# Long convolution and mixture of experts on one core: inputs, filter spectrum, V and U kept in blocks, U's stores in four pieces

## The chip, the core and the metric

The kernel runs on one core of a Trainium2 chip. Its time is the device time of one execution in microseconds (us). The core has a matrix engine (TensorE, "PE" in the profile, its weight loads "PEld"), a vector engine (VectorE, "DVE"), a scalar engine (ScalarE, "ACT"), a general engine (GpSimd, "POOL") and a sequencer for transfers (SyncE, "SP"). Sixteen DMA engines move data between the chip's memory (DRAM, HBM) and the on-chip SBUF of 128 partitions. PSUM holds the sums of TensorE.

## The reference

A causal long convolution by FFT, and then a layer of eight experts, in which each token goes to the one with the largest gate:

```
B, S, D = 8, 5696, 128                  # 45568 tokens
Xf = rfft(x, 2*S, axis=1);  Hf = rfft(h, 2*S, axis=0)
y  = irfft(Xf * Hf, 2*S)[:, :S]         # (B, S, D)
x  = y.reshape(B*S, D)
e  = argmax(x @ w_gate)                 # E = 8 experts
out[t] = gate[t] * (relu(x[t] @ w1[e]) @ w2[e])     # F = 1024
```

## The kernel before

The sequence index is split in two, s = i + 48 m with 48 values of i (NB) and 119 of m (MB, padded to 120), and so is the transform. The batches are worked in three groups of 2, 3 and 3 (SPLIT). Each group passes three stages, with a scratch tensor in DRAM between two of them:

- **A** (`steps_a`, L267): for each four i and each batch a tile xt of 120 x 512 is loaded (L292), split into two parts by ScalarE and POOL or VectorE (xc, L283 and L284), and transformed over m by TensorE (L305). The result ut, 120 frequencies q on the partitions, is copied from PSUM (L319), and when all batches of the group are in it, it is stored to U (L298, after `late` has held it for two steps). Two of these ut belong to each four i: c = 0 for the real part, c = 1 for the imaginary part.
- **B** (`phase_b`, L443): for each block of four q the tile uq (96 rows: c and i; four q; all columns) is loaded from U (L461) with the matrices mt (L453). TensorE transforms over i (L517), VectorE multiplies with the filter's spectrum hh (L529 to L538), POOL adds (L544), TensorE transforms back (L553) with the matrices mi, and vt is stored to V (L603). In group 0 hh is computed on the way and saved to HS, and mi is made from mt by transposition; groups 1 and 2 load hh from HS (L468) and mi from the input miq (L464).
- **C** (`phase_c`, L679): vq is loaded from V with q on the partitions (L696), the last transform gives y, and each token is gated, ranked and scattered into the sorted tensor SR (L644).

The experts (`pipeline`, L1244) read the sorted rows in tiles of 256 tokens as soon as a part is complete, with weights that `weights` (L228) has split beforehand from moe_w1 and moe_w2 into WD, and scatter the results to out (L1220).

The order is written out by hand: each stage is a generator, and `run` (L1322) interleaves them by given costs while the program is built. The program then holds one fixed row of instructions for each engine, and each engine works its row in order. Stage A of group 0 runs with the filter's own transform (`phase_h`) and `weights`; A of groups 1 and 2 runs as a guest inside C of the group before (`Guest`, L350). All plain transfers are issued by SP in its row; the scatters by POOL. The program has eight counters for SP's transfers (DMAHW0 to DMAHW7), which they take in turn. Buffers that matter here: five xt, four ut (two for each c), four vq or uq.

Of the kernel before, what the change touches and what calls it, by code (L numbers as in the profile page):

```python
# [13 lines left out]
F32 = mybir.dt.float32  # L14
# [9 lines left out]
NB = 48  # L24
MB = 119
QN = 120
MP = 120
HP = 64
# [9 lines left out]
SPLIT = (2, 3, 3)  # L38
C3 = (False, True, True)
SLOTS = (6, 6, 6)  # L40
# [36 lines left out]
def conv_moe(ctx: ExitStack, tc: tile.TileContext, I, out, B, S, D, E, F, split):  # L77
    nc = tc.nc
    P = 128
    K2 = 2 * NB  # L80
# [10 lines left out]
    dram = pool("dram", 1, DRAM)  # L91
# [40 lines left out]
    class Group:  # L132
        def __init__(self, g, b0, nb):
            self.g, self.b0, self.nb = g, b0, nb
            self.cols = nb * D
            self.nch = -(-self.cols // 512)
            self.cb = nb // self.nch
            self.cw = self.cb * D
            assert self.cb * self.nch == nb
            self.ni = SLOTS[g] // nb  # L140
            while NB % self.ni:
                self.ni -= 1
            self.ns = self.ni * nb
            self.scb = 3 if self.ns % 3 == 0 else 2
            self.scw = self.scb * D
            self.qw = max(1, 512 // self.cols)
            self.qb = 4 if self.cols <= 384 else (3 if self.cols <= 512 else 2)
            self.U = dram.tile([QN, K2, self.cols], F32, name=f"U{g}")
            self.V = dram.tile([QN, K2, self.cols], F32, name=f"V{g}")

    groups, parts = [], []
# [13 lines left out]
        groups.append(gr)  # L165
    for pt in parts[:-1]:
        pt.filled = True
    HS = dram.tile([NB, 2, QN, D], F32, name="HS")
    WD = dram.tile([4, E * P, F], F32, name="WD")

    fcs = const.tile([MP, 2, QN], F32, name="c_fcs")
# [56 lines left out]
    def weights():  # L228
        hf = F // 2
        raws, late = {}, []  # L230

        def load(n):
            if n >= 2 * E:
                return
            e, k = divmod(n, 2)
            raws[n] = sb.tile([P, F], F32, tag="wb", name=f"wraw{n}", bufs=4)
            if k == 0:
                nc.sync.dma_start(raws[n], I["moe_w1"][e])
            else:
                nc.sync.dma_start(  # L240
                    raws[n].rearrange("p (c d) -> p c d", d=D),
                    I["moe_w2"][e].rearrange("(c p) d -> p c d", p=P),
                )

        yield 4000
        load(0)
        for n in range(2 * E):
            e, k = divmod(n, 2)
            load(n + 1)
            raw = raws.pop(n)  # L250
            for u in range(2):
                yield 1500
                sp = sb.tile([P, 2, hf], F32R, tag="hs", name=f"wsp{n}_{u}", bufs=4)
                rh = raw[:, u * hf : (u + 1) * hf]
                nc.scalar.copy(sp[:, 0, :], rh)
                rest_of[0].tensor_tensor(out=sp[:, 1, :], in0=rh, in1=sp[:, 0, :].bitcast(F32), op=ALU.subtract)
                yield 1500
                while late:
                    nc.sync.dma_start(*late.pop(0))
                dst = WD[2 * k + u, e * P : (e + 1) * P, :]  # L260
                late.append((dst, sp.bitcast(F32).rearrange("p a f -> p (a f)")))
        yield 1500
        while late:
            nc.sync.dma_start(*late.pop(0))
        state["prepped"] = True

    def steps_a(gr, tag, bufs):  # L267
        g, nb = gr.g, gr.nb
        srcs = [(I["x"][gr.b0 + b], b) for b in range(nb)]
        tw = 4 * D  # L270
        items = []
        for ig in range(NB // 4):
            for src, b in srcs:
                items.append((ig, src, b))
        xts, uts, xss = {}, {}, {}
        split = A3[g]

        def cut(n):
            if not split or n >= len(items):
                return  # L280
            xt = xts.pop(n)
            xs = sb.tile([MP, 2, tw], F32R, tag="us", name=f"xc{g}_{n}", bufs=2)
            nc.scalar.copy(xs[:, 0], xt)  # L283
            getattr(nc, ALO[g]).tensor_tensor(out=xs[:, 1], in0=xt, in1=xs[:, 0].bitcast(F32), op=ALU.subtract)  # L284
            xss[n] = xs

        def load(n):
            if n >= len(items):
                return
            ig, src, b = items[n]  # L290
            xts[n] = sb.tile([MP, tw], F32, tag="xt", name=f"xt{g}_{n}", bufs=5)
            nc.sync.dma_start(xts[n], src[:, ig * tw : (ig + 1) * tw])  # L292

        banks, late, clock = {}, [], [0]

        def flush(everything=False):
            while late and (everything or late[0][0] <= clock[0] - 2):
                nc.sync.dma_start(*late.pop(0)[1:])  # L298

        def transform(m):  # L300
            n, c = divmod(m, 2)
            banks[m] = ps.tile([P, 512], F32, tag="cx", name=f"pa{g}_{n}_{c}", bufs=4)
            ops = [(fcs[:, c], xts[n])] if not split else [(fcr[:, u, c], xss[n][:, v]) for u, v in PASSES]
            for k, (lhs, rhs) in enumerate(ops):
                done = nc.tensor.matmul(banks[m][:QN, :], lhs, rhs, start=(k == 0), stop=(k == len(ops) - 1))  # L305
            if c == 1:
                (xss if split else xts).pop(n)
            return done.ins

        def store(m):  # L310
            n, c = divmod(m, 2)
            clock[0] = m
            ig, src, b = items[n]
            if b == 0:
                uts[c] = sb.tile([QN, 4, gr.cols], F32, tag=tag, name=f"ut{g}_{ig}_{c}", bufs=bufs)
            srcv = banks.pop(m)[:QN, :].rearrange("p (i d) -> p i d", d=D)
            lo = c * NB + ig * 4
            cp = nc.scalar.copy if c == 0 else nc.vector.tensor_copy
            cp(uts[c][:, :, b * D : (b + 1) * D], srcv)  # L319
            if b == nb - 1:  # L320
                late.append((m, gr.U[:, lo : lo + 4, :], uts[c]))

        def fetch():
            for n in range(4):
                load(n)

        def begin(m):
            if m % 2 == 0:
                load(m // 2 + 4)
                cut(m // 2 + 1)  # L330
            return transform(m)

        return fetch, cut, begin, store, flush, 2 * len(items)
# [58 lines left out]
    def phase_h():  # L392
# [3 lines left out]
        for k in range(4):  # L396
            n = NB // 4
            yield 1000
            nc.sync.dma_start(
                ht[:, k * n : (k + 1) * n].rearrange("p i d -> p (i d)"), I["h"][:, k * n * D : (k + 1) * n * D]  # L400
            )
        ucs, banks, hcs = {}, {}, {}

# [39 lines left out]
    def phase_b(gr, guest=None):  # L443
# [4 lines left out]
        def load_m(qb):  # L448
            q = qb * QB
            if q >= QN:  # L450
                return
            mt = sb.tile([K2, QB, P], F32, tag="xt", name=f"mt{g}_{q}", bufs=5)
            nc.sync.dma_start(mt, I["mq"][:, q : q + QB])  # L453
            mats[qb] = mt

        def load(qb):
            q = qb * QB
            if q >= QN:
                return
            uq = sb.tile([K2, QB, gr.cols], F32, tag="ld", name=f"uq{g}_{q}", bufs=LD if g else 3)  # L460
            nc.sync.dma_start(uq, gr.U[q : q + QB].rearrange("q p c -> p q c"))  # L461
            mi = mibufs[qb % 4]
            for k in range(2 if g else 0):
                nc.sync.dma_start(mi[k * HP : k * HP + NB], I["miq"][k * NB : (k + 1) * NB, q : q + QB, :])  # L464
            if g != 0:
                hhs[qb] = hhbufs[qb % 3]
                for k in range(2):
                    nc.sync.dma_start(hhs[qb][k * HP : k * HP + NB, :, :QB], HS[:, :, q : q + QB])  # L468
            tiles[qb] = (uq, mi)

        mats, hhs, hbank = {}, {}, {}
# [16 lines left out]
        def filt(qb, k0):  # L488
            if g != 0 or qb * QB >= QN:
                return  # L490
            mt = mats[qb]
            if k0 == 0:
                hbank[qb] = ps.tile([P, QB, D], F32, tag="mh", name=f"hp{g}_{qb}", bufs=2)
            nc.tensor.matmul(hbank[qb][:, k0, :], mt[:, k0, :], uht[:, qb * QB + k0], start=True, stop=True)

        def filt_save(qb, m):
            if qb not in hbank:
# [6 lines left out]
            nc.scalar.copy(hh[k * HP : (k + 1) * HP, c2], hp[c2 * HP : (c2 + 1) * HP])  # L504
            if m == 3:
                hbank.pop(qb)
                late.append((clock[0], HS[:, :, qb * QB : qb * QB + QB], hh[:NB, :, :QB]))

        def forward(n):
            q, c = items[n]  # L510
# [168 lines left out]
    def phase_c(gr, guest=None, after=None):  # L679
# [12 lines left out]
        def load(n):  # L692
            if n >= nu:
                return
            vq = sb.tile([QN, 2, NI, gr.cols], F32, tag="ld", name=f"vq{g}_{n}", bufs=LD)
            nc.sync.dma_start(vq, gr.V.rearrange("q (c i) x -> q c i x", c=2)[:, :, n * NI : (n + 1) * NI, :])  # L696
            vqs[n] = vq.rearrange("q c i x -> q c (i x)")

        nsub = ns // cb
# [740 lines left out]
```

## Time and profile before

| | |
|---|---|
| median of 3 runs | 2229.18 us (2226.16 to 2232.99) |
| the profiled execution's own time | 2210.35 us |
| its span | 2208.6 us |
| PE busy | 2068.3 us, 94% |
| VectorE, ScalarE, POOL busy | 70%, 50%, 58% |
| DMA | 486.04 MB, mean 220 GB/s |

The span lies a little within the execution's own time. Times in the views count from the span's start. A stretch A:B is a part of the span; "x" with a number counts instructions. A row of waits names the waiting engine and line, what it waited for, the sum, how often, and the longest. In the order of time of SP a number is the time that issuing takes, not the transfer.

### The profile page before, as it was taken

To read this page: it belongs to the slowest core of one execution; us is meant where nothing else is said; L and a number is where in the kernel's file an instruction comes from. 1 tells how busy PE (TensorE), PEld (TensorE's weight loads), DVE (VectorE), ACT (ScalarE), POOL (GpSimd) and SP (SyncE) were. 2 spreads that over 40 slices of the span, in tenths; PEclk is the share of its full clock that TensorE was granted. 3 is DMA by queue.
4 is the path that set the end of the run, shared out by engine and by line. 5 is a ranking of instruction groups with operands and counts; after the bars stand their busy time and mean duration, and the time that the engine had idled before them with its cause. 6 is when DMAs were issued, how large, how long until landed. Compare 5 with 4: busy or idle time off the path is not lost. (4 is left out here: it accounts for less than half of the span.)

```text
span 2208.6 us, 47032 instructions
## 1 busy us (share of the span) xinstructions
PE 2068.3 (94%) x14198; PEld 1749.8 (79%) x14198; DVE 1555.7 (70%) x3731; ACT 1103.8 (50%) x2359; POOL 1287.0 (58%) x1486
## 2 busy tenths in 40 slices
PE   7899899699999999989999999999998999999997
PEld 5688655466667888876777778988888999999997
DVE  4588745599987788769987885777764555555554
ACT  4588644233334666643443445555544444445453
POOL 5366548776654288882665661688873444444442
PEclk9999999799999999999999999999999999999998
DMA  9989999699997798978898977777644543444430
GB/s 289 298 284 317 319 342 319 181 282 274 272 277 223 232 284 241 260 210 214 247 262 222 258 241 207 201 201 200 190 154 144 165 146 116 147 143 146 140 126 27
DMA packets 255353, 486.04 MB, mean 220 GB/s; under 512 B 33285, under 2 KB 155266, under 8 KB 255099
## 3 DMA queue, kind: packets, MB, share of 16 engines
q1 hardware_dynamic: 231163, 435.93, 66.4%
q0 software_dynamic: 23936, 47.09, 6.9%
q8 instruction: 115, 1.88, 0.4%
q14 instruction: 139, 1.14, 0.2%
HBM read 593.26 MB, written 173.52 MB: 347 GB/s over the span
## 5 line engine op out<-in xcount | busy, mean ns | idle before, releaser
L1152 DVE SCALAR_TENSOR_TENSOR hs<-mh,hs 128x512 fp32r<-128x512 f32 x728 | 501.1, 691 | 389.8 <-ACT hs L1150 384.8
L1144 PE MATMUL mh<-xtb,wb 128*128 128x256 f32 x4368 | 689.9, 294 | 40.5 <-DMA wb<-WD 28.1
L1144 PEld LDWEIGHTS mh<-xtb,wb 128*128 128x128 f32 x4368 | 585.3, 190 | 110.1 <-issue 45.9
L1150 ACT ACTIVATE hs<-mh 128x512 fp32r<-128x512 f32 x728 | 435.0, 598 | 473.1 <-PE mh L1144 465.6
L1165 PE MATMUL ma<-hs,wb 128*128 128x256 f32 x4368 | 654.0, 286 | 7.3 <-DMA wb<-WD 7.2
L1165 PEld LDWEIGHTS ma<-hs,wb 128*128 128x128 f32 x4368 | 567.3, 190 | 8.9 <-DMA wb<-WD 8.5
L644 POOL DMA_INDIRECT SR<-rt,pi x384 | 401.6, 1046 | 195.9 <-PE pa L305 50.5
L1220 POOL DMA_INDIRECT out<-xr x252 | 245.8, 975 | 334.4 <-DVE xr L1183 282.1
L544 POOL TENSOR_TENSOR zt<-zt,xs 128x384 f32<-128x384 f32 (+1 forms) x280 | 297.3, 1071 | 116.5 <-DVE xs L536 84.4
L568 ACT COPY vt<-vp 96x384 f32<-96x384 f32 (+1 forms) x300 | 148.9, 496 | 349.4 <-PE vp L553 342.7
L553 PE MATMUL vp<-zt,mi 128*96 128x384 f32 (+1 forms) x720 | 259.4, 456 | 8.3 <-DVE xs L536 5.4
L517 PE MATMUL xp<-uq,mt 96*128 96x384 f32 (+1 forms) x720 | 261.9, 460 | 2.3 <-ACT vt L568 1.7
L529 DVE TENSOR_TENSOR zt<-xp,hh 128x384 f32<-128x384 f32 (+1 forms) x300 | 174.1, 580 | 58.5 <-PE xp L517 54.4
L553 PEld LDWEIGHTS vp<-zt,mi 128*96 128x96 f32 x720 | 113.2, 163 | 102.1 <-issue 53.0
L1220 POOL DMA_INDIRECT out<-xb x112 | 109.0, 973 | 140.9 <-ACT hs L1150 118.6
L536 DVE SCALAR_TENSOR_TENSOR xs<-xp,hh 64x384 f32<-64x384 f32 (+1 forms) x300 | 175.7, 586 | 6.1
L305 PE MATMUL pa<-xc,fcr 120*120 120x512 f32 x576 | 166.0, 419 | 14.5 <-ACT xc L283 6.3
L534 DVE TENSOR_TENSOR xs<-xp,hh 64x384 f32<-64x384 f32 (+1 forms) x300 | 173.2, 577 | 6.0
L638 POOL TENSOR_TENSOR c_fcs<-c_fcs 120x64 f32<-120x64 f32 (+2 forms) x384 | 156.0, 406 | 11.4
L517 PEld LDWEIGHTS xp<-uq,mt 96*128 96x128 f32 x720 | 123.7, 195 | 33.0 <-issue 12.8
L305 PEld LDWEIGHTS pa<-xc,fcr 120*120 120x120 f32 x576 | 98.2, 186 | 50.1 <-DVE rk L852 8.5
L319 DVE COPY ut<-pa 120x512 f32<-120x512 f32 x96 | 65.9, 687 | 91.1 <-PE pa L305 81.7
(128 smaller groups left out, 2299.0 us busy)
## 6 DMA issues: line engine op xcount, KB each, us to landing
wb<-WD SPq DMA_DIRECT2D x728, 512.0 KB
vq<-V SPq DMA_DIRECT2D x64, 720.0 KB
U<-ut SPq DMA_DIRECT2D x48, 720.0 KB
uq<-U SPq DMA_DIRECT2D x60, 576.0 KB
V<-vt SPq DMA_DIRECT2D x60, 576.0 KB
xr<-SR SPq DMA_DIRECT2D x182, 130.0 KB
xt<-x SPq DMA_DIRECT2D x96, 240.0 KB
hh<-HS SPq DMA_DIRECT2D x120, 192.0 KB
```

What stands on the lines that cost most here:

```text
L305: done = nc.tensor.matmul(banks[m][:QN, :], lhs, rhs, start=(k == 0), stop=(k == len(ops) - 1))
L517: nc.tensor.matmul(xj, mt[:, k0 + j, :], uc.rearrange("p (b d) -> p b d", d=D), start=True, stop=True)
L529: nc.vector.tensor_tensor(out=zt, in0=x3, in1=hv[:, 0].broadcast_to([P] + wide), op=ALU.mult)
L536: nc.vector.scalar_tensor_tensor(out=xs[to], in0=x3[at], scalar=-1.0, in1=him, op0=ALU.mult, op1=ALU.mult)
L544: eng.tensor_tensor(out=zt, in0=zt, in1=xs, op=ALU.add)
L553: nc.tensor.matmul(vp[:K2, j * cw : (j + 1) * cw].rearrange("p (b d) -> p b d", d=D), mi[:, k0 + j, :], zt.rearrange("p b (j d) -> p b j d ...
L644: s = nc.gpsimd.indirect_dma_start(out=SR[:, :], out_offset=IndirectOffsetOnAxis(ap=pi[:, b : b + 1], axis=0), in_=rt[:, b, :], in_offset= ...
L1144: nc.tensor.matmul(hp[:, u, :], wb[:, a, f, :], xt[:, b, :], start=(n == 0), stop=(n == 2))
L1150: done = nc.scalar.activation(hs[:, 0], hp, AF.Relu)
L1152: nc.vector.scalar_tensor_tensor(out=hs[:, 1], in0=hp, scalar=0.0, in1=hs[:, 0].bitcast(F32), op0=ALU.max, op1=ALU.subtract)
L1165: nc.tensor.matmul(accs[t], wb[:, a, f, :], hs[:, b, u, :], start=(k == 0 and u == 0 and n == 0), stop=(k == NPAIR - 1 and u == 1 and n == 2),
L1220: sc = nc.gpsimd.indirect_dma_start(out=out[:, :], out_offset=IndirectOffsetOnAxis(ap=xr[:, s, D + 1 : D + 2].bitcast(I32), axis=0), in_=x ...
```

## The change

Every tensor in DRAM that a stage reads is laid out in the order of the reads, so that what one transfer reads is one block, or one run per partition. For the inputs x, h, mq, miq and moe_w2 the host does it. HS and U become blocks of four q. In groups 1 and 2 the rows of V are put in another order by the columns of miq, so that a vq tile reads one run of each partition; group 0 reads V as before. U's block has the four q next to each other, while ut has q on the partitions: the columns of fcs are permuted so that partitions 0 to 29 hold the first of each four frequencies, 30 to 59 the second, and so on, and ut is stored in four transfers of 30 partitions.

```diff
-            self.U = dram.tile([QN, K2, self.cols], F32, name=f"U{g}")
+            self.U = dram.tile([QN // 4, K2, 4, self.cols], F32, name=f"U{g}")
-    HS = dram.tile([NB, 2, QN, D], F32, name="HS")
+    HS = dram.tile([QN // 4, NB, 2, 4, D], F32, name="HS")
...
-                    I["moe_w2"][e].rearrange("(c p) d -> p c d", p=P),
+                    I["moe_w2"][e].rearrange("p (c d) -> p c d", d=D),
...
-            nc.sync.dma_start(xts[n], src[:, ig * tw : (ig + 1) * tw])
+            nc.sync.dma_start(xts[n], src[ig])
...
-                late.append((m, gr.U[:, lo : lo + 4, :], uts[c]))
+                n = QN // 4
+                for k in range(4):
+                    late.append((m, gr.U[:, lo : lo + 4, k], uts[c][k * n : (k + 1) * n]))
...
-            nc.sync.dma_start(mt, I["mq"][:, q : q + QB])
+            nc.sync.dma_start(mt, I["mq"][qb])
-            nc.sync.dma_start(uq, gr.U[q : q + QB].rearrange("q p c -> p q c"))
+            nc.sync.dma_start(uq, gr.U[qb])
-                nc.sync.dma_start(mi[k * HP : k * HP + NB], I["miq"][k * NB : (k + 1) * NB, q : q + QB, :])
+                nc.sync.dma_start(mi[k * HP : k * HP + NB], I["miq"][qb, k])
-                    nc.sync.dma_start(hhs[qb][k * HP : k * HP + NB, :, :QB], HS[:, :, q : q + QB])
+                    nc.sync.dma_start(hhs[qb][k * HP : k * HP + NB], HS[qb])
...
-            nc.sync.dma_start(vq, gr.V.rearrange("q (c i) x -> q c i x", c=2)[:, :, n * NI : (n + 1) * NI, :])
+            if g:
+                nc.sync.dma_start(vq.rearrange("q c i x -> q (c i) x"), gr.V[:, 2 * n * NI : 2 * (n + 1) * NI, :])
+            else:
+                nc.sync.dma_start(vq, gr.V.rearrange("q (c i) x -> q c i x", c=2)[:, :, n * NI : (n + 1) * NI, :])
...
+    fcs = fcs[:, :, q.reshape(QN // 4, 4).T.ravel()]
...
-        "x": xp.reshape(B, MP, NB * D),
+        "x": xp.reshape(B, MP, NB // 4, 4 * D).transpose(2, 0, 1, 3),
-        "moe_w2": moe_w2,
+        "moe_w2": moe_w2.reshape(E, F // 128, 128, D).transpose(0, 2, 1, 3).reshape(E, 128, -1),
-        "mq": mqf.transpose(1, 0, 2),
+        "mq": mqf.reshape(QN // 4, 4, 2 * NB, 128).transpose(0, 2, 1, 3),
```

The row of SP in stage A of group 0, before, with the counter or engine that each transfer waits for; xt_8 to xt_11 are tiles of x, ut_1_0 and ut_1_1 the two results of the second four i:

```order
L292 DMA xt_8_210<-x 120x512 [waits DMAHW1_49,Pool_49]
L292 DMA xt_9_226<-x 120x512 [waits DMAHW2_49,Pool_49]
L298 DMA U_70<-ut_1_0_185 120x1024 [waits DMAHW3_49,Activation_49]
L298 DMA U_70<-ut_1_1_198 120x1024 [waits DMAHW4_49,DVE_49]
L292 DMA xt_10_247<-x 120x512 [waits DMAHW5_49,Pool_49]
L292 DMA xt_11_277<-x 120x512 [waits DMAHW6_49,Pool_49]
```

The same place of SP's row in the changed kernel:

```order
L292 DMA xt_8_216<-x 120x512 [waits DMAHW7_49,Pool_49]
L292 DMA xt_9_232<-x 120x512 [waits DMAHW0_49,Pool_49]
L298 DMA U_70<-ut_1_0_185 30x4x256 [waits DMAHW1_49,Activation_49]
L298 DMA U_70<-ut_1_0_185 30x4x256 [waits DMAHW2_49]
L298 DMA U_70<-ut_1_0_185 30x4x256 [waits DMAHW3_49]
L298 DMA U_70<-ut_1_0_185 30x4x256 [waits DMAHW4_49]
L298 DMA U_70<-ut_1_1_201 30x4x256 [waits DMAHW5_49,DVE_49]
L298 DMA U_70<-ut_1_1_201 30x4x256 [waits DMAHW6_49]
L298 DMA U_70<-ut_1_1_201 30x4x256 [waits DMAHW7_49]
L298 DMA U_70<-ut_1_1_201 30x4x256 [waits DMAHW0_49]
L292 DMA xt_10_259<-x 120x512 [waits DMAHW1_49,Pool_49]
L292 DMA xt_11_289<-x 120x512 [waits DMAHW2_49,Pool_49]
```

Two transfers have become eight; a counter comes round after eight transfers, so the one before it must have landed; the places around them are the same.

SP in C of group 0 with A of group 1 (ut of 120 x 1536, vq a tile of V), before:

```order
L298 DMA U_72<-ut_4_0_3004 120x1536
L298 DMA U_72<-ut_4_1_3006 120x1536
L292 DMA xt_21_3308<-x 120x512
L696 DMA vq_9_3340<-V_71 120x2x768
L292 DMA xt_22_3357<-x 120x512
```

The same place in the changed kernel:

```order
L298 DMA U_72<-ut_4_0_3094 30x4x384 x4
L298 DMA U_72<-ut_4_1_3096 30x4x384 x4
L292 DMA xt_21_3410<-x 120x512
L701 DMA vq_9_3442<-V_71 120x2x768
L292 DMA xt_22_3459<-x 120x512
```

Here too two stores have become eight, between the same loads.

## Rows read from the trace of the kernel before

**Rows 1.** Stretches: busy us (instructions) PE, PEld, DVE, ACT, POOL; PEclk, DMA share, GB/s
```profile
0.00:88.00 88.00, 70.52 (x321) 51.67 (x321) 41.47 (x60) 48.23 (x94) 49.10 (x51) 0.94 0.91 298
98.00:262.00 164.00, 155.42 (x854) 130.26 (x855) 130.08 (x188) 127.34 (x232) 95.82 (x76) 0.95 0.95 302
262.00:395.00 133.00, 114.98 (x598) 69.00 (x596) 69.76 (x307) 64.38 (x160) 83.03 (x120) 0.96 0.94 317
434.00:690.00 256.00, 246.99 (x1207) 167.06 (x1207) 242.68 (x466) 90.20 (x200) 163.71 (x177) 0.99 0.99 270
700.00:945.00 245.00, 235.55 (x1749) 203.63 (x1749) 190.16 (x628) 157.07 (x360) 167.69 (x219) 0.99 0.86 250
990.00:1320.00 330.00, 318.38 (x1814) 241.61 (x1813) 293.89 (x555) 130.67 (x270) 177.96 (x185) 0.99 0.87 242
1740.00:2140.00 400.00, 400.00 (x3430) 400.00 (x3430) 226.02 (x397) 199.26 (x395) 191.91 (x198) 1.00 0.42 139
```

**Rows 2.** What SP waited for, 0 to 88: us, times, longest
```profile
SPq L292 <- POOL xc L284: 18.9, 9, 4.7
SPq L298 <- ACT ut L319: 5.2, 2, 3.2
SPq L298 <- DVE ut L319: 4.7, 3, 2.4
```

**Rows 3.** Order of time on SP, 59 to 70: start, us taken, transfer
```profile
59.28 0.79 SPq L298 DMA_DIRECT2D U<-ut  x2
60.17 3.13 SPq L292 DMA_DIRECT2D xt<-x  x2
...
64.12 2.45 SPq L298 DMA_DIRECT2D U<-ut  x2
66.67 2.97 SPq L292 DMA_DIRECT2D xt<-x  x2
69.73 0.83 SPq L298 DMA_DIRECT2D U<-ut  x2
```

**Rows 4.** Single lines: SP's issues, ns min/median/max, first and last start
```profile
L298 SPq DMA_DIRECT2D U<-ut x72: 316/360/2807, 14.5 to 954.1; - x72
...
L292 SPq DMA_DIRECT2D xt<-x x96: 324/426/5950, 1.3 to 918.9; - x96
...
L603 SPq DMA_DIRECT2D V<-vt x90: 312/537/1270, 124.9 to 1331.9; - x90
...
L468 SPq DMA_DIRECT2D hh<-HS x120: 543/547/807, 435.5 to 1295.3; - x120
...
L696 SPq DMA_DIRECT2D vq<-V x64: 843/933/2846, 268.2 to 1580.2; - x64
```

**Rows 5.** The page, DMA issues: transfer, count, KB each
```profile
U<-ut SPq DMA_DIRECT2D x48, 720.0 KB
...
hh<-HS SPq DMA_DIRECT2D x120, 192.0 KB
...
U<-ut SPq DMA_DIRECT2D x24, 480.0 KB
```

**Rows 6.** DMA queue, 741.6 to 744, U stores: packets, MB, share
```profile
q1 hardware_dynamic: 161, 0.87, 94.4%
```

**Rows 7.** DMA queue, 475.8 to 476.4, expert weights
```profile
q1 hardware_dynamic: 73, 0.26, 105.3%
```

**Rows 8.** DMA queue, 474 to 474.6, uq and V
```profile
q1 hardware_dynamic: 153, 0.24, 105.7%
```

**Rows 9.** DMA queue, 193.6 to 194.4, uq and V of group 0
```profile
q1 hardware_dynamic: 240, 0.25, 97.7%
```

**Rows 10.** DMA queue, 198.8 to 199.6, w2
```profile
q1 hardware_dynamic: 421, 0.24, 101.5%
```

**Rows 11.** DMA queue, 711.6 to 713.6, V loads
```profile
q1 hardware_dynamic: 160, 0.45, 97.4%
```

**Rows 12.** DMA queue, 471 to 473, hh loads mostly
```profile
q1 hardware_dynamic: 278, 0.43, 96.8%
```

More of the change, by code (lines that the diff above doesn't have):

```diff
@@ L268, in steps_a @@
         g, nb = gr.g, gr.nb
-        srcs = [(I["x"][gr.b0 + b], b) for b in range(nb)]
+        srcs = [(I["x"][:, gr.b0 + b], b) for b in range(nb)]
         tw = 4 * D
@@ L399, in phase_h @@
             nc.sync.dma_start(
-                ht[:, k * n : (k + 1) * n].rearrange("p i d -> p (i d)"), I["h"][:, k * n * D : (k + 1) * n * D]
+                ht[:, k * n : (k + 1) * n].rearrange("p i d -> p (i d)"), I["h"][k]
             )
@@ L493, in filt @@
                 hbank[qb] = ps.tile([P, QB, D], F32, tag="mh", name=f"hp{g}_{qb}", bufs=2)
-            nc.tensor.matmul(hbank[qb][:, k0, :], mt[:, k0, :], uht[:, qb * QB + k0], start=True, stop=True)
+            nc.tensor.matmul(hbank[qb][:, k0, :], mt[:, k0, :], uht[:, k0 * (QN // QB) + qb], start=True, stop=True)
         def filt_save(qb, m):
@@ L506, in filt_save @@
                 hbank.pop(qb)
-                late.append((clock[0], HS[:, :, qb * QB : qb * QB + QB], hh[:NB, :, :QB]))
+                late.append((clock[0], HS[qb], hh[:NB]))
         def forward(n):
@@ L1393 @@
     mqf = mq.astype(f32)
+    miq = np.stack([mqf[:, :, :NB], mqf[:, :, HP : HP + NB]], 2)
+    ni = SLOTS[1] // SPLIT[1]
+    miq = miq.reshape(QN, 2, NB // ni, ni, 2, NB).transpose(0, 2, 1, 3, 4, 5).reshape(QN // 4, 4, 2 * NB, 2, NB)
     total = (B * S - E) // T + E
@@ L1422 @@
     ins = {
-        "x": xp.reshape(B, MP, NB * D),
-        "h": hp.reshape(MP, NB * D),
+        "x": xp.reshape(B, MP, NB // 4, 4 * D).transpose(2, 0, 1, 3),
+        "h": hp.reshape(MP, 4, NB // 4 * D).transpose(1, 0, 2),
         "moe_w1": moe_w1,
-        "moe_w2": moe_w2,
+        "moe_w2": moe_w2.reshape(E, F // 128, 128, D).transpose(0, 2, 1, 3).reshape(E, 128, -1),
         "fcs": fcs.astype(f32),
-        "mq": mqf.transpose(1, 0, 2),
-        "miq": np.concatenate([mqf[:, :, :NB], mqf[:, :, HP : HP + NB]], 2).transpose(2, 0, 1),
+        "mq": mqf.reshape(QN // 4, 4, 2 * NB, 128).transpose(0, 2, 1, 3),
+        "miq": miq.transpose(0, 3, 4, 1, 2),
         "small": small,
```

## Prediction

> **What bounds the kernel now.** I read the table of stretches first, then what SP waited for, its order of time in the first stage, and last the pace of single kinds of transfers.
>
> In stretches [rows 1]: TensorE (PE) is busy 400.00 of 400 us from 1740 to 2140, when only the experts run. No transfer can shorten that. Before it come stage A of group 0 (0 to 88 us), B of group 0 (98 to 262), C of group 0 with A of group 1 as its guest (262 to 395), B of group 1 (434 to 690), C of group 1 with A of group 2 (700 to 945), B of group 2 (990 to 1320) and C of group 2. The change acts in these. In the two stretches in which U is written first, the DMA engines are busy 0.91 and 0.94, while PE is idle 17.5 of 88 us and 18.0 of 133. In B of group 0 PE is busy 155.4 of 164, in B of group 1 VectorE 242.7 of 256, in B of group 2 PE 318.4 of 330, in C of group 1 PE 235.6 of 245. So where U is read a compute engine is already at 95 to 96%, and where U is written the transfers set the pace.
>
> SP issues every transfer of this kernel but the scatters, in one fixed order. In the first stage it waits mostly for compute: 18.9 us for POOL to free an xt buffer, some 10 us for ut to be filled [rows 2]. In its order of time a turn of two x tiles and two U stores takes about 5.6 us there (59.28 to 64.12 to 69.73), and the xt loads hold SP some 1.5 us each (3.13 and 2.97 us for two) [rows 3], against 0.43 for such an issue in the middle [rows 4]. SP is held when the engines are behind: the sign of a stage at the transfers' limit.
>
> **The change part by part.** On PE, VectorE, ScalarE and POOL nothing moves: their instructions stand in the same order, and their durations don't depend on which row is which frequency. On SP a U store becomes four, nothing else changes place.
>
> *Issue.* There are 24 U stores in each group (24 of 480 KB, 48 of 720 KB [rows 5]), so 72 more issues per group. No row shows a store of 30 partitions. The nearest below is a U store as it is, 0.316 us at least and 0.360 in the middle; the nearest above are the V store, which also writes four runs per partition, 0.537, and the hh load, 0.547 [rows 4]. I take 0.54, since the V store has the same form. That is 96 x 0.54 - 24 x 0.36 = 43 us more of SP's time in each of the three stretches; at 0.32 it would be 22. Back come 0.933 - 0.43 = 0.5 us for each of the 48 V loads of groups 1 and 2 (24 us), and about 0.1 us for each of 120 hh loads and 30 HS stores (15 us), all off the path in stretches where SP has time.
>
> *Engine time.* A transfer's pace is its MB over the length of the window over the share. U stores of 6144 B runs go at 0.87 / 2.4 / 0.944 = 384 GB/s [rows 6], 4096 B at 0.26 / 0.6 / 1.053 = 411 [rows 7], 1536 B at 0.24 / 0.6 / 1.057 = 378 [rows 8], 1024 B at 0.25 / 0.8 / 0.977 = 320 [rows 9], 512 B at 0.24 / 0.8 / 1.015 = 296 [rows 10]. The share of rows 6 is just over 15/16: a transfer of 120 partitions sits on 15 engines, and a piece of 30 may too; so I scale by 15/16 or 16/15 where the kinds differ.
> - U written: group 0 moves 24 x 480 KB = 11.8 MB, now in 1024 B runs: 39.3 us instead of 30.6, 8.7 more. Groups 1 and 2 move 17.7 MB each, in 1536 B runs: 50.0 instead of 46.1, 3.9 more each.
> - U read is the mirror image: group 0 has 11.8 MB in 4096 B runs, 8.2 us less; groups 1 and 2 have 17.7 MB each in 6144 B runs at 410 GB/s, 3.6 less each.
> - w2: 8 x 512 KB in 4096 B runs instead of 512 B: 4 us less, half in A and half in B of group 0.
> - V loads go at 0.45 / 2 / 0.974 = 231 GB/s in 3072 B runs [rows 11], slower than any store, so it is not the run length that holds them back. I take no gain; at the pace of rows 6 the 24 loads of a group, 17.7 MB, would take 46 us instead of 77, the other end, and in C of group 1 PE could use at most its 9.4 idle us of that.
> - The blocks of x, h, mq and miq keep their run lengths. hh and HS go from 2048 to 4096 B, at most a fifth of small amounts. I cost both at nothing; B's compute hides it.
>
> Over the whole kernel the engines' time is a wash (8.7 + 7.8 - 8.2 - 7.2 - 4 = 3 us less). What counts is the place: more where transfers bind, less where compute does.
>
> The Trainium skill ("DMA: Bandwidth & Descriptors", Rules for kernel authors) speaks against this change: small transfers are to be coalesced into one, and splitting one by partition halves brings nothing, since the parts run on the same engines. Here B of group 1, with its 192 KB hh loads [rows 5], still keeps the engines at 0.99 [rows 1], so the trace agrees only in part. By the page's fit of 2 us for each transfer and eight in flight, 216 more would cost, as an estimate, 54 us; the sum goes by the rows above.
>
> *Stage by stage.* A of group 0: SP has to issue 96 pieces (51.8 us) and 41 others at 0.43 (17.6), 69 of 88 us, and waits 29 us for compute as now [rows 2]; with the waits kept in full it ends at 69 + 29 = 98, 10 us late, and with 0.1 us behind each of 137 issues, as between the lines of rows 3, 24 us late. If they are hidden by SP being late itself, nothing is lost there. The engines' 8.7 - 2 = 6.7 us more would just fill their idle tenth (0.91 to 0.99). A turn needs 8 x 0.54 + 2 x 0.43 + 0.43 = 5.6 us of SP, all of the turn of rows 3. Behind the late pieces stand the next xt loads, for which ScalarE's and POOL's cuts wait, then PE. I take 8 us, from 0 to 24. C of group 0: the engines, at 0.94, get 3.9 us more, and pieces that each wait for the transfer eight before them let less be queued while SP waits. I take 5, from 2 to 15. C of group 1: 43 us more of SP in 245, the engines at 0.86; weight loads may stand 4.3 us behind a pair of stores. I take 2, from -9 to 8. B of group 0: 10 us less for the engines (8.2 + 2), but PE is idle only 8.6 us; I take 2 off, at most 8. B of groups 1 and 2: one off each, at most 13 and 12, the idle time of VectorE and of PE there.
>
> Sum: 8 + 5 + 2 - 2 - 2 = 11 us more. The profiled execution took 2210.35 us around a span of 2208.6, so 2221; it lies 19 us under the median of the three runs, 2229.18. On the median: 2240 us.
>
> **The rivals.**
> 1. *The relief in B wins, the kernel is faster.* If the idle time in the three B stages is mostly waiting for transfers, and SP absorbs the pieces (0.32 us each), B gives back 6 + 8 + 6 of its 8.6, 13.3 and 11.6 idle us, A and C lose 8: 12 us less, 2217. For it: the engines are at 0.95 and 0.99 in the first two. Against it: the waits of SP show compute late, not transfers. It decides once B gives back more than the 8 us.
> 2. *Nothing to see.* The pieces are issued within SP's waits, the swap of run lengths cancels: 2229, give or take 5. For it: the sum of engine time is unchanged, and SP's waits are long.
> 3. *Narrow pieces are slow.* The loads of hh, into 48 partitions, go at 0.43 / 2 / 0.968 = 222 GB/s in 2048 B runs [rows 12]. If stores of 30 partitions do too, U takes 53 us instead of 31 in A and 80 instead of 46 in C: some 22 + 30 more (the idle 0.06 of C takes a few us of 34), with C of group 1 hiding its 34 in its idle seventh: 2281. Against it: rows 12 are writes into SBUF and a U store reads it; for it: nothing in the trace isolates a narrow store.
>
> **How the numbers follow.** My forecast 0.42, rival 1 0.20, rival 2 0.22, rival 3 0.16. A change under 0.3% (7 us) cannot be told from none here: faster is below 2222, slower above 2236. Faster 0.2, same 0.22, slower 0.58. The likeliest one's own range is 2232 to 2260. The ends of the stages add up to -40 and +47, but they hardly fall together; the range takes in the first rival and reaches towards the third, which leaves one in ten on each side: 2213 to 2272.
>
> **What would show it.** In the changed profile the U pieces should take SP about 0.54 us each; SP should wait less for POOL's xc in the first 90 us; the first uq load should come up to 10 us later than now; C of group 0 should end some 5 us later still; the B stages should last the same to 2 us with the DMA share down a few hundredths; and PE should run the experts in the end as it does now. If the stretch from the first uq load of group 0 to its last V store is over 5 us shorter, rival 1 holds. If A's engines show far more time per byte of U, rival 3. If A is no longer than before, my main term is wrong.

## The result and the profile after

| | before | after |
|---|---|---|
| median, same chip | 2230.45 us (2226.16 to 2232.99, 6 runs) | 2244.40 us (2240.66 to 2247.58, 6 runs) |
| the profiled execution | 2210.35 us | 2240.93 us |
| its span | 2208.6 us | 2239.1 us |

The changed kernel is slower: the recorded ratio is 1.0075, 95% interval [1.0057, 1.0093]; the medians, 14 us apart, give 1.0063. Here and below the two can differ by about 0.1%. 2240 us was forecast. The two profiled executions lie 30 us apart, twice as far as the medians. Before's median was 2230 us in these runs, and 2228, 2210 and 2231 us on the three chips of the experiments. The profiled execution of before, 2210 us, lies outside the range of its six runs and at the median of the second of those chips, so the rows of before above may come from another chip than those of after. Stage times are therefore compared further below between two kernels profiled on one chip.

The stretches of after, as in [rows 1] (busy us of PE, PEld, DVE, ACT, POOL; clock, DMA share, GB/s):

```profile
0.00:88.00 88.00, 69.46 (x304) 50.57 (x304) 39.31 (x57) 44.66 (x87) 47.71 (x49) 0.92 0.92 280
262.00:395.00 133.00, 103.75 (x514) 62.44 (x513) 65.45 (x263) 59.89 (x147) 75.90 (x108) 0.94 0.97 301
1800.00:2140.00 340.00, 340.00 (x2879) 335.87 (x2877) 189.57 (x332) 164.35 (x332) 160.96 (x167) 1.00 0.42 140
```

The first two are the stretches in which U is written first. The DMA engines are as busy as before or busier (0.92, 0.97) and move less (280 instead of 298 GB/s, 301 instead of 317). The last shows TensorE without a gap when only the experts run, as before, but from 1800 us on; from 1740 to 1800 it was busy 56.8 of 60.

What SP waited for, 0 to 88, as in [rows 2]:

```profile
SPq L292 <- POOL xc L284: 7.9, 4, 4.6
SPq L298 <- DMA xt<-x: 4.1, 6, 1.4
...
SPq L298 <- DMA ht<-h: 2.6, 1, 2.6
...
SPq L298 <- ACT ut L319: 1.4, 3, 0.7
```

The wait for POOL fell from 18.9 to 7.9 us and that for ScalarE's ut from 5.2 to 1.4. New is that the U stores (L298) wait for earlier transfers, of x, h and the weights. These are not data that they need: by the rows of order above it is the counter, whose last transfer has to land first.

The order of time on SP at the place of [rows 3] (start, us taken):

```profile
61.81 4.69 SPq L298 DMA_DIRECT2D U<-ut  x8
66.60 0.83 SPq L292 DMA_DIRECT2D xt<-x  x2
...
67.96 5.63 SPq L298 DMA_DIRECT2D U<-ut  x8
73.69 0.86 SPq L292 DMA_DIRECT2D xt<-x  x2
74.65 4.69 SPq L298 DMA_DIRECT2D U<-ut  x8
```

Before, the xt loads held SP (3.13 and 2.97 us for two) and two U stores went by in 0.8 to 2.5. Now the eight pieces take 4.69 and 5.63 us, and two xt loads 0.83: the time has moved from waiting for compute to the stores. From one pair of stores to the next it took 4.8 and 5.6 us [rows 3]; now it takes 6.2 and 6.7 (61.81 to 67.96, 67.96 to 74.65).

SP's issues by line, as in [rows 4] (ns min/median/max), each from its own line's view:

```profile
L298 SPq DMA_DIRECT2D U<-ut x288: 311/422/1891, 14.4 to 976.6; - x144
...
L699 SPq DMA_DIRECT2D vq<-V x48: 18/409/1467, 723.3 to 1603.4; - x48
...
L470 SPq DMA_DIRECT2D hh<-HS x120: 253/362/1239, 454.8 to 1317.9; - x120
```

A piece takes 0.42 us in the middle; I had taken 0.54. The V loads of groups 1 and 2 went from 0.93 to 0.41, as forecast, and hh from 0.55 to 0.36, nearly twice the gain that was forecast.

The queue of after in 0.8 us (66.0 to 66.8) in which only pieces of group 0 move, and in 1 us (945 to 946) with pieces of group 2 (packets, MB, share):

```profile
q1 hardware_dynamic: 314, 0.28, 102.4%
```

```profile
q1 hardware_dynamic: 257, 0.35, 95.2%
```

That is 0.28 / 0.8 / 1.024 = 342 GB/s in runs of 1024 B and 0.35 / 1 / 0.952 = 368 in runs of 1536 B, beside 320 and 378 for other transfers in runs of that length [rows 9, 8] and 384 for a whole store in runs of 6144 B [rows 6]. Stores of thirty partitions, several of them in flight, are not slow.

### The profile page after: what moved, and what is told of

Read it like the earlier page. It is cut to its first block, busy times and chain, and to the rows that moved or that the text cites. A ratio compares the mean times of both kernels' runs of the same rounds, so it can differ in the third digit from the quotient of the medians.

```text
span 2239.1 us, 47291 instructions
## 1 busy us (share of the span) xinstructions
PE 2080.9 (93%) x14198; PEld 1753.4 (78%) x14198; DVE 1556.1 (69%) x3731; ACT 1101.4 (49%) x2359; POOL 1285.8 (57%) x1486
## 5 line engine op out<-in xcount | busy, mean ns | idle before, releaser
L1225 POOL DMA_INDIRECT out<-xb x112 | 109.2, 975 | 169.7 <-ACT ot L1180 108.6
```

What stands on the lines that cost most here:

```text
L1225: sc = nc.gpsimd.indirect_dma_start(out=out[:, :], out_offset=IndirectOffsetOnAxis(ap=xr[:, s, D + 1 : D + 2].bitcast(I32), axis=0), in_=x ...
```

## The experiments

My theory: U's stores cost because there are four times as many transfers. It has two forms. In theory 1 the time that SP needs to issue them decides, in theory 2 the eight counters that all transfers share. The rivals: the short runs of U's new layout, and the other blocks.

**U as before, the rest changed.**

```diff
-            self.U = dram.tile([QN // 4, K2, 4, self.cols], F32, name=f"U{g}")
+            self.U = dram.tile([QN, K2, self.cols], F32, name=f"U{g}")
...
-                n = QN // 4
-                for k in range(4):
-                    late.append((m, gr.U[:, lo : lo + 4, k], uts[c][k * n : (k + 1) * n]))
+                late.append((m, gr.U[:, lo : lo + 4, :], uts[c]))
...
-            nc.sync.dma_start(uq, gr.U[qb])
+            nc.sync.dma_start(uq, gr.U[q : q + QB].rearrange("q p c -> p q c"))
...
-            nc.tensor.matmul(hbank[qb][:, k0, :], mt[:, k0, :], uht[:, k0 * (QN // QB) + qb], start=True, stop=True)
+            nc.tensor.matmul(hbank[qb][:, k0, :], mt[:, k0, :], uht[:, qb * QB + k0], start=True, stop=True)
...
-    fcs = fcs[:, :, q.reshape(QN // 4, 4).T.ravel()]
```

> The changed kernel with U alone as before (one store per ut, old layout). Theory (the four pieces cost SP's issues and the counters, the rest of the change does nothing): 2226 to 2233 us, ratio to the kernel before 0.997 to 1.001. Rival (the other blocks are slow too, or shift the stages): ratio 1.004 or more. Rival (the other blocks help and U hides it): ratio under 0.996.

Measured: 2225.02 us (12 runs), 0.998 [0.9961, 0.9999] of before. The loss is U's alone; the other blocks together are worth nothing or a little gain.

**U's change alone** (the same lines of the diff, put into the kernel before).

> The kernel before with the change of U alone. Theory: as slow as the changed kernel or a little slower, ratio 1.005 to 1.010, since only U matters. Rival (the other blocks cause the loss): ratio within 0.002 of 1.

Measured: 2237.73 us (8 runs), 1.0051 [1.0033, 1.0068].

**Four transfers, old layout.** Runs of 6144 and 4096 B as before, U and uq as before.

```diff
-                late.append((m, gr.U[:, lo : lo + 4, :], uts[c]))
+                n = QN // 4
+                for k in range(4):
+                    late.append((m, gr.U[k * n : (k + 1) * n, lo : lo + 4, :], uts[c][k * n : (k + 1) * n]))
```

> The kernel before, U's layout and run lengths unchanged, but each U store in four transfers of 30 partitions. Theory (number of issues): most of the loss, ratio 1.004 to 1.009, the stretch up to the first uq load of group 1 some 10 to 20 us longer. Rival (the short runs cost the engines' time, not the issues): ratio within 0.002 of 1.

Measured: 2241.25 us (6 runs), 1.0057 [1.0036, 1.0078], as much as U's whole change. The first uq load of group 1 comes at 453.5 us, beside 436.6 and 442.2 in the fourth and the first experiment, whose stores are whole.

**One transfer, short runs.** A row of U is padded by 64 floats, so that a store writes four runs per partition.

```diff
-            self.U = dram.tile([QN, K2, self.cols], F32, name=f"U{g}")
+            self.U = dram.tile([QN, K2, self.cols + 64], F32, name=f"U{g}")
...
-                late.append((m, gr.U[:, lo : lo + 4, :], uts[c]))
+                late.append((m, gr.U[:, lo : lo + 4, : gr.cols], uts[c]))
...
-            nc.sync.dma_start(uq, gr.U[q : q + QB].rearrange("q p c -> p q c"))
+            nc.sync.dma_start(uq, gr.U[q : q + QB, :, : gr.cols].rearrange("q p c -> p q c"))
```

> The kernel before with U's rows padded by 256 B, so that each U store is still one transfer but writes four runs of 1024 or 1536 B per partition; the loads keep their run lengths. Theory (number of issues): ratio 1.000 to 1.003 (the engines' 8.7 and 3.9 us hardly seen). Rival (run length): ratio 1.005 or more.

Measured: 2227.71 us (12 runs), 1.0003 [0.9987, 1.0019]. These four ran on one chip (before 2227.69 us) and settle the first question: the number of transfers costs, and the length of their runs does not, or by no more than 0.2%.

**SP's time without counters.** Two loads of a register from SBUF (of a 0 in the tile zero) on SP behind each U store of the kernel before.

```diff
...
+                for _ in range(2):
+                    nc.sync.value_load(zero[0:1, 0:1], min_val=0, max_val=1)
```

> The kernel before; behind each of the 72 U stores SP loads a register twice (some 1.3 us of SP's time, about what three further issues take), with no transfer and no counter. Theory 1 (what the pieces cost is SP's issue time): ratio 1.004 to 1.007, as with four pieces. Theory 2 (what they cost is that a counter comes round after eight small transfers, so SP waits for a landing): ratio under 1.002.

Measured: 2239.18 us (6 runs) against 2210.34, on another chip: 1.0129 [1.0096, 1.0162]. The dose was larger than meant (ns min/median/max of what a load consists of):

```profile
L303 SPq TENSOR_LOAD <-zero x144: 271/742/2446, 15.0 to 987.2; - x144
L303 SPq FUSED_REGOPS  x144: 147/147/192, 15.7 to 988.7; - x144
```

Two loads are 1.8 us a store, where the pieces add 4 x 0.42 - 0.36 = 1.3. So it shows that SP's time costs, and not that it costs as much as the pieces. Its 1.29% cannot be set beside the 0.5 to 0.6% above either: the kernel before is 17 us faster on this chip than on the other, four pieces in all groups were not run here, and in time 2239 us is what the kernels with four pieces took there (2238 and 2241).

**Counters with little time.** Three transfers behind each U store whose condition is never true: they move nothing, but each takes its counter (never[0] is a register that holds 0, SK a scratch tensor).

```diff
...
+                for _ in range(3):
+                    nc.sync.dma_start(SK[skips[0]], ident[0:1, :], cond=never[0], cond_hint=False)
...
```

> The kernel before; behind each of the 72 U stores SP has three transfers that are skipped by a register (0.1 us each, nothing is moved), each of which takes the next of the eight counters. Theory 1 (issue time): 0.4 us a store, a third of the pieces' cost at most, ratio under 1.002. Theory 2 (counters): ratio 1.003 to 1.006, and SP's U lines in C of group 0 take some 4 us or more a store as the pieces do.

Measured: 2241.60 us (6 runs), same chip, 1.0143 [1.0112, 1.0174]. SP's order of time in the first stage:

```profile
64.88 0.75 SPq L308 DMA_DIRECT2D SK<-ident  x3
65.72 0.33 SPq L304 DMA_DIRECT2D U<-ut  x1
66.33 3.80 SPq L308 DMA_DIRECT2D SK<-ident  x3
```

Three of them go by in 0.75 us where nothing holds them; at the next place the same three hold SP 3.80 us, and the profile counts 91 us of waits at this line in the whole program. So waiting for counters costs, too. It is more than either theory expected, but it is not the counters alone: the three take 0.75 us of SP even where they are free.

**Two pieces of 60 partitions**, and **four in group 0 alone** (the split of the third experiment with 2 for 4, and under `if g == 0`).

> The kernel before with each U store in two transfers of 60 partitions, run lengths as before. Theory 1 (issue time, one third of the further issues): ratio about 1.002. Theory 2 (counters: eight transfers still hold more than half of the bytes): ratio 1.000 to 1.002. A cost of any splitting as such would give 1.005 again.

> The kernel before with the U stores of group 0 alone in four transfers, those of groups 1 and 2 whole. By the forecast's sizes A of group 0 carries over half of the loss: ratio 1.003 to 1.005. Rival (the loss is in C of group 0 and of group 1, where the transfers between are long): ratio 1.000 to 1.002.

Measured on that chip: 2212.36 us (12 runs), 1.001 [0.999, 1.003], and 2216.72 (12 runs), 1.0024 [1.0004, 1.0044]. One more transfer per store cannot be told from none. That does not show that the cost is out of proportion to the count: a third of 0.57% is 0.19%, inside the interval, so neither theory is ruled out. With four pieces in group 0 alone the kernel loses about 5 us (1 to 10), between the two expectations. The first transform of B comes at 115.9 us here, beside 109.2 with two pieces.

**One register load, and the changed kernel beside the one with U as before.** One load instead of two; and on the same chip, a third one (before 2230.57 us, 29 runs), the changed kernel and the first experiment again.

> Kernel before, with one register load of 0.9 us (742 + 147 + 18 ns in the run with two) on SP behind each of the 72 U stores, which takes no counter. The three additional pieces of a store take 1.2 to 1.4 us of SP when nothing holds them, so this is about two thirds of their time on SP. Theory 1 (the time that SP spends decides): 0.3 to 0.7% slower, 1.003 to 1.007, half of the 1.3% of two loads or a little more than half of the pieces' 0.6 to 0.75%. Theory 2 (the counters decide, and the two loads cost only because they held SP longer than the pieces do): within 0.15% of before, under 1.0015.

> The changed kernel again, so that it, the kernel with U as before and the kernel before stand on one chip. Both theories: 0.5 to 0.9% over before, and 0.6 to 1.0% over the kernel with U alone as before. If this chip is one on which before takes about 2210 us, the first U load of group 0 should come 4 to 8 us later than in before, and C of group 0 should show the part that the slower chip hid: up to 3 us.

> The changed kernel with U's layout and stores as before, once more, beside the changed kernel on the same chip. If the other blocks are worth what the first run showed, 0.996 to 1.000 of before; if that was chance, the interval lies around 1.000. The gain that my engine-time rows give for w2 is 4 us at most (0.998).

Measured, 12 runs each: one load 2239.75 us, 1.0033 [1.0015, 1.0052]; the changed kernel 2240.08, 1.0044 [1.0028, 1.006]; with U as before 2224.73, 0.9973 [0.9954, 0.9991]. The changed kernel is 0.69% over the one with U as before, as expected, and a little less over the kernel before than the 0.5% expected. The load was a little longer here:

```profile
L303 SPq TENSOR_LOAD <-zero x72: 437/935/1818, 15.5 to 976.3; - x72
L303 SPq FUSED_REGOPS  x72: 111/152/192, 16.1 to 977.2; - x72
```

So 1.1 us of SP's time per store, without any counter, cost 0.33% on the chip on which the pieces, at 1.3 us, cost 0.69%. In proportion to their time the pieces would cost 0.4% by that (an estimate), a little over half. SP's time costs by itself; that it accounts for the whole is not shown. The lower end of the interval, 0.15%, is as much as was expected at most if the counters decide. And the load does not act where the pieces do: the first uq load came at 99.0 us, as with U as before (99.1), with the pieces at 102.8, and some 8 us of the loss of the profiled execution lie in B of group 1 (278.9 us beside 271.0), where no U store and so no register load stands. Why, is open. The expected gain of the other blocks was seen twice, and the version with U as before beats both kernels: by 0.27% [0.09, 0.46] the kernel before, by 15 us of the medians the changed one. Which of the other blocks gives the gain was not tried.

## Why the prediction came out, step by step

The stages of two kernels from one chip: the changed kernel, cut at its last transform in A of group 0, the first of B, the last of B, the first of C, and the first uq or vq load of each later stage:

```profile
0.00:90.80 90.80, 71.86 (x318) 51.63 (x318) 39.96 (x59) 46.65 (x92) 48.64 (x50) 0.94 0.91 278
90.80:115.80 25.00, 15.54 (x91) 13.49 (x89) 9.90 (x16) 11.56 (x23) 3.01 (x3) 0.75 0.93 288
115.80:266.10 150.30, 146.38 (x829) 122.27 (x828) 128.57 (x185) 122.96 (x225) 95.87 (x76) 0.98 0.94 305
...
283.50:453.80 170.30, 133.09 (x674) 80.08 (x674) 78.25 (x390) 67.11 (x173) 107.67 (x161) 0.89 0.85 262
453.80:723.10 269.30, 260.79 (x1308) 179.06 (x1308) 253.31 (x485) 97.77 (x216) 170.87 (x184) 1.00 0.96 271
723.10:998.00 274.90, 259.99 (x1915) 223.63 (x1915) 206.07 (x704) 167.82 (x389) 191.55 (x259) 0.98 0.82 235
```

The same stages with U as before, all else changed (so the two differ in U alone, and w2 and the other blocks are in both):

```profile
0.00:88.20 88.20, 71.64 (x317) 52.17 (x318) 40.99 (x59) 47.37 (x93) 48.74 (x50) 0.94 0.90 295
88.20:109.60 21.40, 15.13 (x90) 13.34 (x89) 9.38 (x16) 10.91 (x22) 2.99 (x3) 0.86 0.96 296
109.60:259.80 150.20, 146.26 (x829) 122.15 (x828) 128.61 (x185) 122.88 (x225) 95.84 (x76) 0.99 0.96 308
...
277.30:436.60 159.30, 127.40 (x674) 77.18 (x674) 79.24 (x390) 67.14 (x173) 107.53 (x161) 0.93 0.83 277
436.60:707.50 270.90, 261.76 (x1315) 179.64 (x1315) 253.89 (x486) 98.29 (x217) 170.77 (x184) 1.00 0.97 270
707.50:979.50 272.00, 258.45 (x1907) 223.43 (x1906) 205.29 (x703) 167.50 (x387) 193.67 (x259) 0.98 0.81 237
```

The second number of a row is the length. The changed kernel is 2.6 us longer in A of group 0, 3.6 in the passage to B, 0.1 in B, 0.1 shorter in the row left out (17.4 against 17.5), 11.0 longer in C of group 0, 1.6 shorter in B of group 1 and 2.9 longer in C of group 1; behind that the two differ by less than 1 us until the end of their spans (2239.1 and 2219.8). These are single executions; the medians differ by 15.4. How far other traces bear them out is said with each stage.

- **A of group 0: 8 forecast, 6.2 measured, and only part of it where I put it.** The uq load was 3.7 us late (102.8 against 99.1), by the mechanism that I gave: pieces at SP, next loads late. The turn of 5.6 us that I set the pieces against was the longer of the two in [rows 3]; the other took 4.8. What I had not priced is the passage. SP of the changed kernel, and then of the one with U as before:

```profile
87.28 9.52 SPq L298 DMA_DIRECT2D U<-ut  x16
...
102.22 0.41 SPq L455 DMA_DIRECT2D mt<-mq  x1
102.82 0.58 SPq L463 DMA_DIRECT2D uq<-U  x1
```

```profile
87.03 2.66 SPq L298 DMA_DIRECT2D U<-ut  x2
...
97.59 0.42 SPq L453 DMA_DIRECT2D mt<-mq  x1
99.14 0.34 SPq L461 DMA_DIRECT2D uq<-U  x1
```

  At 87 us the one has sixteen pieces left, 9.52 us, the other two stores, 2.66. The mt loads behind them come 4.6 us late, and TensorE waits for them, 7.9 us instead of 5.1:

```profile
PE hp L496 <- DMA mt<-mq: 7.9, 1, 7.9
```

```profile
PE hp L494 <- DMA mt<-mq: 5.1, 3, 4.5
```

  This stage is the best shown: the first transform of B comes at 115.1 to 117.0 us in all five traces with four pieces in group 0, and at 108.5 to 109.6 in all five with one store or two, on every chip.
- **Issue of a piece: 0.54 taken, 0.42 measured.** The V store was the wrong neighbour for a store of four runs; a U store as it is (0.36) was nearer. By that 43 us more of SP per group are 96 x 0.42 - 24 x 0.36 = 32. Where the DMA engines are behind, the counters add to it: in C of group 0 eight pieces took 9.47 us.
- **C of group 0: 5 forecast, 11 measured in this pair, some 7 over all traces; this is the term that I sized too small.** From the first transform of C to the start of the uq load it took 164.3 to 170.0 us in the four traces with four pieces in every group (mean 167.7), and 159.0 to 164.0 in the three with whole stores on the chips where before takes about 2230 us (mean 160.7); the two ranges almost touch. I took 3.9 us of engine time for U's shorter runs, and a little for the counters. From the packets of the queue in that stage (their times added up, over 16 engines), U's own engine time is 48.0 us instead of 46.3, so 1.7; but the V loads (3072 B, the same in both) took 40.4 instead of 32.0 us, and x 20.6 instead of 19.1. The middle V packet took 160 ns instead of 121. SP, changed kernel first:

```profile
328.14 0.85 SPq L701 DMA_DIRECT2D vq<-V  x1
329.10 1.03 SPq L292 DMA_DIRECT2D xt<-x  x2
330.22 0.85 SPq L701 DMA_DIRECT2D vq<-V  x1
...
332.32 9.47 SPq L298 DMA_DIRECT2D U<-ut  x8
```

```profile
326.57 4.42 SPq L292 DMA_DIRECT2D xt<-x  x2
331.16 1.03 SPq L298 DMA_DIRECT2D U<-ut  x2
332.29 2.05 SPq L699 DMA_DIRECT2D vq<-V  x1
334.44 5.80 SPq L292 DMA_DIRECT2D xt<-x  x2
```

  With whole stores two transfers of 720 KB are handed over in a microsecond and run beside the loads; with pieces SP stands at the eight of them for 9.47 us, in part until earlier transfers have landed, and the loads behind them come in a bunch. After, V loads with little beside them (384.6 to 386.6 us):

```profile
q1 hardware_dynamic: 140, 0.40, 96.8%
```

  0.40 / 2 / 0.968 = 207 GB/s: with little beside them they are as slow as [rows 11] had it (231) or slower, while their mean over the stage with whole stores among them was 325. That the loads lose because they meet each other and no longer stores is my reading of these rows; the runs show that they lose with pieces (40.7 us in U's change alone, 36.8 with the old layout) and not with short runs (32.5, against 34.1 before). They also show that pieces are not needed for it: with whole stores they took 44.8 us where skipped transfers held SP, and 36.1 with one register load. So holding SP is enough to slow the loads, whatever the form of the stores beside them. What SP waited for in C of group 0 (280 to 454 us, changed kernel; 277 to 437, U as before):

```profile
SPq L298 <- DMA vq<-V: 14.0, 7, 3.2
...
SPq L292 <- DVE xc L284: 9.8, 5, 4.4
```

```profile
SPq L292 <- DVE xc L284: 29.8, 8, 7.1
```

  The stores now wait 14.0 us for the V loads whose counters they take, and the 20 us less that SP waits for xc show it late itself. The copies into ut pay for it: who waited for the stores in the whole program, changed kernel and U as before (us, times):

```profile
ACT ut L319: 28.3, 9
DVE ut L319: 28.0, 10
```

```profile
ACT ut L319: 13.1, 4
...
DVE ut L319: 4.6, 2
```

  Of the 11.0 us, 5.3 are idle time of TensorE (37.2 against 31.9), and 5.7 are busy time for the same 674 matmuls, at a mean granted clock of 0.89 instead of 0.93: of its two levels, 1.2 and 2.4 GHz, TensorE was granted the lower one for longer in the stage with more gaps.
- **C of group 1: 2 forecast, 2.9 measured.** The DMA engines had room there (0.82). Other traces show nothing clear: from the first vq load of group 1 to the first uq load of group 2 it took 270.0 to 275.2 us with pieces and 272.0 to 274.8 with whole stores.
- **B: 2, 1 and 1 us off forecast for groups 0, 1 and 2; 0.1 more, 1.6 less and 0.4 more measured** (2 us of engine time for w2 that I counted in group 0 are in both kernels). As said, PE and VectorE bound it. The contiguous uq brought no relief to be seen: the DMA share in B of group 1 is 0.96 instead of 0.97. Rival 1, the relief in B, is gone with that.
- **w2 and the other blocks: 4 us less of engine time forecast.** Measured for all of them together: 2.7 and 5.8 us less of the medians on two chips. Rival 2, nothing to see, would be near the truth for this half of the change.
- **Rival 3, narrow pieces slow: wrong** by the 342 and 368 GB/s above; it had 222.

So the sum of 11 came from the right mechanism: late loads behind the pieces in A and C of group 0. C of group 0 was too small, the issue time and A a little too large, the relief in B did not come, and the other blocks' gain was a little too small. That the total lies within 3 us of the 14 on the medians is in part luck, since these errors offset each other. The rule of the Trainium skill that I weighed ("DMA: Bandwidth & Descriptors", Rules for kernel authors: do not split by partition) pointed the right way. Its fit of 2 us a transfer (section "Anatomy of one DMA — SWDGE (gpsimd) path") is measured on transfers that GpSimd issues, and these are issued by SP; the estimate of 54 us from it was three and a half to five times the 10 to 15 us that U's pieces cost.

What stays open: how the pieces' cost divides between SP's time and the counters. The two traces from one chip tell how SP's own time divides. 96 pieces at 0.42 us are 40 us of issuing in each group, 24 whole stores at 0.34 are 8. The waits of these lines for earlier transfers add up to 10.8 us instead of 3.7 in A of group 0 and to 22.4 instead of 1.9 in C. So of what SP spends more on the pieces, issuing is 32 us in each group and waiting 7 in A and 20 in C of group 0; how much of either ends up in the kernel's time is not shown. Register loads and skipped transfers each cost by themselves (1.29 and 1.43%), but on a chip on which the pieces were not run in all groups.

## What to carry over

Where one queue issues everything in a fixed order, as here, splitting a store was paid at the next loads in that row, and at the passage between stages, not at the store: count the issues between the last store and the first load of the next stage. Two pieces cost nothing that could be measured here (0.1%, from -0.1 to 0.3) and four did; whether the cost sets in at some point or grows with the count is not shown. A layout that makes reads contiguous is worth it only where the reader waits for its reads; B did not. And compare two edits on one chip: the kernel before differed by 0.9% between chips, as much as the edits cost.

## What the runs showed that I had not expected

- One and the same kernel has medians of 2210.34 and 2230.57 us on two chips, 0.9% apart, more than any edit here but two moved it. The kernels with four pieces in all groups, the register loads or the skipped transfers all take 2238 to 2244 us, whichever the chip; why is open.
- A register load on SP takes 0.9 to 1.1 us with what belongs to it, more than two issues of a transfer.
- A transfer that is skipped still holds SP until its counter is free: three took 0.75 us or 3.80.
- Loads next to split stores got slower by a quarter (V: 32.0 to 40.4 us of engine time) though neither their form nor their bytes changed, and next to whole stores, with SP held by skipped transfers, by more (44.8).
